# Keeping a token's row and its upsampled row side by side in DRAM, and adding them only after the gather

## The chip, the cores and the metric

The kernel runs on one core of a Trainium2 chip. The metric is the device time of one execution in microseconds (us); a single number is the median of several runs. PE is TensorE, DVE is VectorE, ACT is ScalarE, POOL is GpSimd, and SP is the engine whose queue issues most DMAs (SPq).

## The reference

Two stages, cut to what matters:

```
# q, k, v: (8 batches, 8 heads, 576 positions, 64)
q_d, k_d, v_d = means over groups of 4 positions                 # 144 positions
out_up    = repeat(softmax(q_d k_d^T / 8) v_d, 4, axis=positions)
out_local = softmax(q k^T / 8 where |i - j| < 4) v
x = (out_up + out_local) as (4608 tokens, 512)

logits = x @ w_gate                                              # 8 experts
# all (token, expert) pairs in falling order of logit; a token goes to the first
# expert that still has one of its 576 places
out[tokens of e] = relu(x[tokens of e] @ w1[e]) @ w2[e]          # 512 -> 1024 -> 512
```

`out_up` has only 144 different rows per batch: four neighbouring tokens share one. The gate is linear, so the logits of `x` are those of `out_local` plus those of `out_up`.

## The kernel before

**Attention.** The 4608 tokens are 36 tiles `u` of 128 tokens (4.5 tiles per batch). For a tile, `loc_s`, `loc_t` and `loc_v` compute the local attention with PE, and `norm` leaves it in SBUF as `x` (128 x 512). For a batch `b`, two passes `g` of four heads compute the attention of the 144 coarse positions; their `end()` writes it to a DRAM tensor `up_dram`: 128 of the 144 rows as two DMAs (L387, one per `g`), the other 16 rows as one (L394). Later `load_up` (L416) reads, for each tile, the 32 coarse rows that it needs, each four times, into an SBUF tile `up`. `log_a` (L484) adds: `x = x + up`, on DVE for the first 28 tiles and on POOL for the last 8. `store` (L487) writes the sum to `x_dram` (4608 x 512). `log_t` transposes it on PE (L494, four 128x128 blocks in fp32) and splits it into two fp16 parts (ACT L498, DVE L499); `log_m` multiplies them with the gate's weights (L509, L512) and DVE sums the result into `lg` (L514).

The order of this stage is written out by hand: every step of tile `u` has a lag in the table `LOC`, the steps are sorted by time, and each engine gets its instructions in that order. All DMAs of the stage share SP's queue: stores, loads of `up`, the q, k and v of the next batch (`nat`, `natt`, L200 and L215) and the windows of v (`vw`, L229).

**Routing.** The token-expert assignment takes a fixed number of threshold searches: DVE compares (L703), PE counts (L733). Those for the first expert stand between the stages, those for a later expert run beside the matmuls of the one before. Each ends with `idx`, 576 row numbers, as four columns of 128 and one of 64.

**Experts.** A scheduler orders this stage, with priorities. For an expert, `gather` lets POOL issue five indirect DMAs (L1068) that fetch rows of `x_dram` into `xg`. For the first two experts PE transposes `xg` (L1077, four blocks per 128 rows) and ACT and DVE split it into two fp16 parts `xt`; for the others ACT and DVE split first, into a tile `xs` (L1088 is DVE's part), and a DMA transposes it (L1090). The weights are split into fp16 parts too (L1053 is DVE's part). Then come the two layers, `pH` (L1105) and `pX` (L1134), and POOL scatters the rows of `y` to the output (L1143).

Of the kernel before, what the change touches and what calls it, by code (L numbers as in the profile page):

```python
# [49 lines left out]
LOC = {'up': 1.7, 'st': 4.6, 't': 1.3, 'lm': 8.07, 's0': 0.33, 's1': 0.331, 'lt': 5.61, 'v0': 1.83, 'v1': 1.831, 'add': 4.5}  # L50
# [39 lines left out]
class Attention:  # L90
    def __init__(self, ctx, tc, q, k, v, wg, ident, identb, maskc, x_dram, up_dram, lg, big, more=()):
        self.tc, self.nc = tc, tc.nc
        self.q, self.k, self.v = q, k, v
        self.x_dram, self.up_dram, self.lg = x_dram, up_dram, lg
# [22 lines left out]
        self.vw, self.vd, self.qz, self.qdz, self.qdt, self.sw, self.ptw = [], [], [], [], [], [], []  # L117
        self.sd = cst.tile([128, 9, G], F32, name="sd")
# [245 lines left out]
    def down_v(self, b, g):  # L364
# [10 lines left out]
        x = self.wk.tile([128, 5, D], F32, name="xu", bufs=2)  # L375
# [8 lines left out]
        def end():  # L384
            r = self.norm(o, x[:, :4], 4 + g, 4.0)
            up = self.up_dram[b * G:b * G + 128, 256 * g:256 * g + 256]
            nc.sync.dma_start(up, x[:, :4].rearrange("p h d -> p (h d)"))  # L387
            if g:
                own = self.wk.tile([128, 2], F32, name="own")
                nc.vector.tensor_tensor(own, r[:, 4:].to_broadcast([128, 2]), self.half, op=OP.mult)  # L390
                y = x[:, 4]
                nc.vector.tensor_scalar(y, o[:, 260:324], own[:, :1], None, op0=OP.mult)
                nc.vector.scalar_tensor_tensor(y, o[:, 325:389], own[:, 1:], y, op0=OP.mult, op1=OP.add)
                nc.sync.dma_start(bass.AP(tensor=up.tensor, offset=up.offset - 256 * g + 128 * HD,  # L394
                                          ap=[[D, H], [HD, 16], [1, D]]), y)
# [14 lines left out]
    def load_up(self, u):  # L410
        for b in {4 * u // NW, (4 * u + 3) // NW}:
            for g in range(2):
                self.need(("v", b, g))
        t = self.wk.tile([128, HD], F32, name="up", bufs=UB)
        src = self.up_dram[32 * u:32 * u + 32]
        getattr(self.nc, UPQ).dma_start(t, bass.AP(tensor=src.tensor, offset=src.offset, ap=[[HD, 32], [0, 4], [1, HD]]))  # L416
        self.up[u] = t

# [59 lines left out]
    def log_a(self, u):  # L481
        nc = self.nc
        x = self.x[u]
        (nc.gpsimd if u >= ADDU else nc.vector).tensor_tensor(x, x, self.up[u], op=OP.add)  # L484

    def store(self, u):
        getattr(self.nc, STQ).dma_start(self.x_dram[128 * u:128 * u + 128], self.x[u])  # L487

    def log_t(self, u):
        nc = self.nc  # L490
        x = self.x[u]
        p = self.ps.tile([128, 4, 128], F32, name="g", bufs=8)
        for c in range(4):
            nc.tensor.transpose(p[:, c], x[:, 128 * c:128 * c + 128], self.ident)  # L494
        xt = self.wk.tile([128, 2, 4, 128], F16, name="xt", bufs=TB)
        pf = p.rearrange("p c t -> p (c t)")
        hi = xt[:, 0].rearrange("p c t -> p (c t)")
        nc.scalar.activation(hi, pf, AF.Copy, scale=XS)  # L498
        self.after(FT, lambda: nc.vector.scalar_tensor_tensor(xt[:, 1].rearrange("p c t -> p (c t)"), pf, XS, hi,  # L499
                                                              op0=OP.mult, op1=OP.subtract), ("x", u))  # L500
        self.xt[u] = xt

    def log_m(self, u):
        nc = self.nc
        self.need(("x", u))
        xt = self.xt.pop(u)
        l = self.ps.tile([128, 2, E], F32, name="g", bufs=8)
# [6 lines left out]
        nc.vector.tensor_reduce(self.lg[:, u], l.rearrange("p s e -> p e s"), axis=AX.X, op=OP.add)  # L514
# [23 lines left out]
    def run(self, after, ready):  # L538
        self.so, self.x, self.up, self.xt, self.ptd = {}, {}, {}, {}, {}
# [13 lines left out]
        for b in range(B):  # L553
# [35 lines left out]
        for u in range(NT):  # L589
            if u > 1:  # L590
                work.append((u - VWT, 0, 0, lambda u=u: self.load_vw(u), False))
            for j, (name, lag) in enumerate(LOC.items()):
# [4 lines left out]
                if name == "up":  # L597
                    at = max(at, end[(4 * u + 3) // NW])
                work.append((at, 2, j, stage[name](u), name in PEL))
                if name == "lm" and u in SETUP:  # L600
                    steps = after(SETUP[u], u + 1)
                    work += [(at + SPACE * k, 3, k, lambda g=steps: next(g, None), False) for k in range(24)]
# [23 lines left out]
XSB = 4  # L626
# [381 lines left out]
class Experts:  # L1008
# [50 lines left out]
    def gather(self, idx, first):  # L1059
# [5 lines left out]
        for c, (s0, n) in enumerate(SL):  # L1065
            xg = self.wk.tile([128, HD], F32, name="xg", bufs=5)
# [4 lines left out]
            xgs.append(xg)  # L1071

        def piece(c):
            s0, n = SL[c]
            p = self.ps.tile([128, 4, 128], F32, name="pX", bufs=2)
            for d in range(4):
                self.turned = nc.tensor.transpose(p[:, d, :n], xgs[c][:n, 128 * d:128 * d + 128], self.ident[:n, :n])  # L1077
# [5 lines left out]
        def piece_dma(c):  # L1083
            s0, n = SL[c]
            xs = self.wk.tile([128, 2, HD], F16, name="xs", bufs=XSB)
            with self.tc.high_priority():
                nc.scalar.activation(xs[:n, 0], xgs[c][:n], AF.Copy, scale=XM)
            getattr(nc, LOE).scalar_tensor_tensor(xs[:n, 1], xgs[c][:n], XM, xs[:n, 0], op0=OP.mult, op1=OP.subtract)  # L1088
# [4 lines left out]
        return xt, piece if first else piece_dma  # L1093

    def mlp(self, w, xt, idx, in1, in2):
# [28 lines left out]
        for c, (s0, n) in enumerate(SL):  # L1124
# [13 lines left out]
            y = self.wk.tile([128, 512], F32, name="y", bufs=3)  # L1138
# [152 lines left out]
```

## Time and profile before

| | |
|---|---|
| median of 3 runs | 795.96 us (794.89 to 797.41) |
| the profiled execution | 787.11 us, of which 785.1 us are the span |
| attention, to the last logits | about 0 to 292 us of the span |
| routing for the first expert, up to its gather | 292 to 322 us |
| eight experts | 322 to 785 us |
| PE busy | 679.8 us, 87% of the span |
| DVE busy | 560.6 us, 71% |
| POOL busy | 244.6 us, 31% |

A row of the profile names the line of the kernel, the engine, the operation and its tiles (out<-in), then how often it ran, its busy time, the mean duration of one, and the idle time of its engine just before it. A row that starts with SPq is SP's DMA queue. All times within the run are on the scale of the span.

### The profile page before, as it was taken

The page shows a single profiled execution, that of the slowest core. Times are in us where ns is not written, and L with a number is a line of the kernel's source. Part 1 is how long each engine was busy: PE and PEld are TensorE (multiplying, and loading weights), DVE is VectorE, ACT ScalarE, POOL GpSimd, SP SyncE. Part 2 cuts the span into 40 slices and gives each one's busy share as a digit, 9 for nine tenths or more (in the row PEclk, how much of TensorE's full clock was granted, in tenths as well). Part 3 has the DMA queues.
Part 4 walks back from the last instruction along what each step waited for, and adds up shares of the span by engine and source line. Part 5 has one row for each costly group of instructions (what it writes and reads, how often), then busy time and mean ns, then how long its engine had stood idle before and what let it go on. Part 6 is the DMA issues. An engine that isn't in the chain of part 4 may idle for free.

```text
span 785.1 us, 21193 instructions
## 1 busy us (share of the span) xinstructions
PE 679.8 (87%) x8565; PEld 470.0 (60%) x8565; DVE 560.6 (71%) x1679; ACT 331.6 (42%) x631; POOL 244.6 (31%) x274
## 2 busy tenths in 40 slices
PE   7687988886898863399899999999999979999994
PEld 4576777675777752365466466366466456574752
DVE  7878879977797887887969979798889336171210
ACT  3357677663776440341624325144234134262210
POOL 9263455535346440300610502121320402201001
PEclk9699899998999995599999999999999989999998
DMA  9949979798999750621615555572835935404001
GB/s 258 220 132 242 255 193 287 194 262 209 226 238 214 190 178 10 196 80 51 252 34 196 139 168 171 101 257 67 257 114 215 222 120 128 108 2 100 22 27 34
DMA packets 148133, 125.00 MB, mean 159 GB/s; under 512 B 92228, under 2 KB 122436, under 8 KB 148036
## 3 DMA queue, kind: packets, MB, share of 16 engines
q1 hardware_dynamic: 140656, 102.12, 49.3%
q0 software_dynamic: 6432, 20.98, 8.8%
q8 instruction: 68, 1.11, 0.6%
q10 hardware_dynamic: 948, 0.55, 0.3%
q14 instruction: 29, 0.24, 0.1%
HBM read 95.30 MB, written 21.23 MB: 148 GB/s over the span
## 4 chain that ended last, share of the span: by engine, by line
PE 32%; DVE 23%; issue 21%; DMA 11%; ACT 5%; POOL 3%; SPq 3%; POOLq 0%; ACTq 0%; DVEq 0%
PE pH L1105 10%; PE pX L1134 5%; DVE cmp L703 2%; POOL out_dram L1143 2%; DVE wl L1053 2%; PE g L292 2%; DMA nat<-in_q_dram 2%; PE pR L733 2%; PE g L476 2%; DMA vw<-in_v_dram 2%; DMA up_dram<-xu 2%; DMA nat<-in_moe_w_dram 1%; DVE ht L1121 1%; PE g L373 1%; DMA xt<-xs 1%
## 5 line engine op out<-in xcount | busy, mean ns | idle before, releaser
L1105 PE MATMUL pH<-xt,wh 128*128 128x256 f16 (+1 forms) x1024 | 199.3, 289 | 5.4 <-DMA xt<-xs 4.7
L1134 PE MATMUL pX<-wh,ht 128*128 128x512 f16 (+1 forms) x640 | 182.4, 384 | 1.9 <-DVE xt L1081 1.9
L1105 PE MATMUL pH<-xt,wl 128*128 128x320 f16 (+1 forms) x512 | 147.7, 289 | 0.0
L1134 PEld LDWEIGHTS <-ht 128*128 128x128 f16 (+1 forms) x960 | 82.2, 101 | 90.2 <-issue 6.4
L1143 POOL DMA_INDIRECT out_dram<-y,idx x40 | 44.1, 1102 | 280.2 <-ACT y L1140 224.0
L1134 PE MATMUL pX<-wl,ht 128*128 128x512 f16 (+1 forms) x320 | 119.2, 384 | 0.0
L1105 PEld LDWEIGHTS <-wh 128*128 128x128 f16 x1024 | 98.5, 99 | 32.5 <-issue 8.3
L1118 ACT ACTIVATE ht<-pH 128x512 f16<-128x512 f32 (+1 forms) x128 | 45.5, 408 | 129.8 <-PE pH L1105 129.8
L1053 DVE SCALAR_TENSOR_TENSOR wl<-nat,wh 128x512 f16<-128x512 f32 x128 | 84.7, 682 | 2.8 <-ACT wh L1051 0.6
L1068 POOL DMA_INDIRECT xg<-x_dram,idx x40 | 49.4, 1234 | 112.0 <-DVE idx L1004 33.9
L1121 DVE SCALAR_TENSOR_TENSOR ht<-pH,ht 128x512 f16<-128x512 f32 (+1 forms) x128 | 52.5, 450 | 41.1 <-ACT ht L1118 40.7
L1140 ACT ACTIVATE y<-pX 128x512 f32<-128x512 f32 (+1 forms) x40 | 23.7, 594 | 127.0 <-PE pX L1134 82.2
L1051 ACT ACTIVATE wh<-nat 128x1024 f16<-128x1024 f32 x64 | 66.6, 1056 | 9.5 <-DMA nat<-in_moe_w_dram 9.5
L1105 PEld LDWEIGHTS <-wl 128*128 128x128 f16 x512 | 50.5, 99 | 12.4
L465 ACT COPY pt<-g 64x512 f32<-64x512 f32 x72 | 41.8, 580 | 35.5 <-PE g L454 34.4
L292 PE MATMUL g<-ident,nat 128*128 128x128 f32 x256 | 40.7, 287 | 14.7 <-DMA nat<-in_q_dram 12.3
L476 PE MATMUL g<-vw,pt 128*64 128x65 f32 x1152 | 45.4, 232 | 3.3 <-ACT pt L465 2.1
L1142 DVE SCALAR_TENSOR_TENSOR y<-pX,y 64x512 f32<-64x512 f32 x8 | 5.5, 693 | 59.2 <-ACT y L1140 59.0
L476 PEld LDWEIGHTS g<-vw,pt 128*64 128x64 f32 x1152 | 40.4, 145 | 9.4 <-ACT pt L465 5.7
L278 ACT COPY kt<-g 64x512 f32<-64x512 f32 (+1 forms) x56 | 35.1, 626 | 19.2 <-PE g L292 11.0
L265 POOL TENSOR_TENSOR gtmp<-qz 64x576 f32<-64x576 f32 x28 | 32.6, 1163 | 30.0 <-DVE kdt L268 24.7
L278 ACT COPY qz<-g 64x512 f32<-64x512 f32 (+1 forms) x52 | 33.0, 634 | 19.6 <-PE g L292 16.5
(219 smaller groups left out, 1190.3 us busy)
## 6 DMA issues: line engine op xcount, KB each, us to landing
nat<-in_moe_w_dram SPq DMA_DIRECT2D x28, 1024.0 KB
vw<-in_v_dram SPq DMA_DIRECT2D x136, 96.0 KB
up<-up_dram SPq DMA_DIRECT2D x36, 256.0 KB
x_dram<-x SPq DMA_DIRECT2D x36, 256.0 KB
nat<-in_q_dram SPq DMA_DIRECT2D x16, 512.0 KB
nat<-in_k_dram SPq DMA_DIRECT2D x16, 512.0 KB
nat<-in_v_dram SPq DMA_DIRECT2D x14, 512.0 KB
up_dram<-xu SPq DMA_DIRECT2D x16, 128.0 KB
```

What stands on the lines that cost most here:

```text
L278: self.nc.scalar.copy(out, in_)
L292: nc.tensor.transpose(p[:, a, :, fp], src[:, 4 * hh + 2 * a + s, 2 * fp:2 * fp + 2].rearrange("p f d -> p (f d)"), self.ident)
L465: self.nc.scalar.copy(out, in_)
L476: nc.tensor.matmul(o[64 * i:64 * i + 64, 65 * h:65 * h + 65], pt[:, 2 * g + i, h].rearrange("p b q -> p (b q)"), self.vw[u % 4][:, i, 4 * ...
L1051: nc.scalar.activation(hi, r, AF.Copy, scale=sc)
L1053: nc.vector.scalar_tensor_tensor(lo[:, a:a + LOP], r[:, a:a + LOP], sc, hi[:, a:a + LOP], op0=OP.mult, op1=OP.subtract)
L1068: self.fetched = nc.gpsimd.indirect_dma_start(out=xg[:n], out_offset=None, in_=self.x, in_offset=bass.IndirectOffsetOnAxis(ap=idx[:n, c:c ...
L1105: mm = nc.tensor.matmul(p[:, s, :s1 - s0], w[d][a][:, 128 * f:128 * f + 128], xt[:, b, d, s0:s1], start=j == 0, stop=j == len(seq) - 1)
L1118: last = nc.scalar.activation(hi, q, AF.Relu)
L1121: nc.vector.scalar_tensor_tensor(lo, q, 0.0, hi, op0=OP.max, op1=OP.subtract)
L1134: mm = nc.tensor.matmul(p[o:o + m], ht[:, f, h0:h0 + m], w[4 + f // 2][b][:, 512 * (f % 2):512 * (f % 2) + 512], start=j < parts, stop=j > ...
L1143: i = nc.gpsimd.indirect_dma_start(out=self.out, in_=y[:n], in_offset=None, out_offset=bass.IndirectOffsetOnAxis(ap=idx[:n, c:c + 1], axis=0))
```

## The change

A row of `x_dram` now has 1024 numbers: the local attention on the left, the upsampled row on the right. Nothing in the attention stage adds the two any more.

- The coarse attention of a batch is collected in `xu` (128 x 512) and `yu` (the last 16 rows). `up_put` writes `xu` with one DMA, each row to four tokens (1 MB), and `yu` with four DMAs. `up_dram`, `load_up` and `log_a` are gone.
- The gate is applied to the coarse rows once: `up_t` and `up_m` are `log_t` and `log_m` for the 128 rows of `xu`. The 16 rows per batch in `yu` are read back from `x_dram` in two groups, of five and three batches (`tail_get`), and go the same way. The logits go to a small DRAM tensor `lup_dram`, four copies each (`lup_put`: 32 bytes per token), and come back in the layout of `lg` with two DMAs (`lget`: tiles 0 to 23 and 24 to 35). `ladd` adds them to `lg`, the first on POOL, the second on DVE.
- The lags are new, `x` has 4 buffers instead of 6, and the first of two preparations of the routing starts two tiles earlier.
- The gather of an expert fetches 4 KB rows. For the first expert PE sums while it transposes: two fp32 matmuls with the identity per block, accumulated, in place of one transpose. For the others POOL adds the halves (128 x 512) behind the gathers. From the third expert on, `xs` lies in the right half of `xg`. The output tile `y` has 2 buffers instead of 3.

```diff
-        up = self.up_dram[b * G:b * G + 128, 256 * g:256 * g + 256]
-        nc.sync.dma_start(up, x[:, :4].rearrange("p h d -> p (h d)"))
...
+        at = d.offset + b * S * 2 * HD + HD
+        self.nc.sync.dma_start(bass.AP(tensor=d.tensor, offset=at, ap=[[8 * HD, 128], [2 * HD, 4], [1, HD]]),
+                               x[:, None].to_broadcast([128, 4, HD]))
+        for r in range(4):
+            self.nc.sync.dma_start(bass.AP(tensor=d.tensor, offset=at + (512 + r) * 2 * HD,
+                                           ap=[[D, H], [8 * HD, 16], [1, D]]), y)
...
+        self.logits_t(self.xu[b][0], ("up", b), "xtu", 2)
...
+        self.nc.sync.dma_start(bass.AP(tensor=d.tensor, offset=d.offset + at * E, ap=[[4 * E, n], [E, 4], [1, E]]),
+                               rows[:, None].to_broadcast([n, 4, E]))
...
+        (self.nc.vector if u1 == NT else self.nc.gpsimd).tensor_tensor(a, a, b, op=OP.add)
...
-        (nc.gpsimd if u >= ADDU else nc.vector).tensor_tensor(x, x, self.up[u], op=OP.add)
...
-LOC = {'up': 1.7, 'st': 4.6, 't': 1.3, 'lm': 8.07, 's0': 0.33, 's1': 0.331, 'lt': 5.61, 'v0': 1.83, 'v1': 1.831, 'add': 4.5}
+LOC = {'st': 3.4, 't': 1.3, 'lm': 5.46, 's0': 0.33, 's1': 0.331, 'lt': 3.0, 'v0': 1.83, 'v1': 1.831}
...
+            xg = self.wk.tile([128, 2 * HD], F32, name="xg", bufs=5)
...
+        if how:
+            for c, (s0, n) in enumerate(SL):
+                with self.tc.high_priority():
+                    nc.gpsimd.tensor_tensor(xgs[c][:n, :HD], xgs[c][:n, :HD], xgs[c][:n, HD:], op=OP.add)
...
+                if how == 0:
+                    nc.tensor.matmul(p[:, d, :n], cut, self.ident[:n, :n], start=True, stop=False)
+                    self.turned = nc.tensor.matmul(p[:, d, :n], xgs[c][:n, HD + 128 * d:HD + 128 * d + 128],
+                                                   self.ident[:n, :n], start=False, stop=True)
+                else:
+                    self.turned = nc.tensor.transpose(p[:, d, :n], cut, self.ident[:n, :n])
```

The lines of the changed kernel that the order below names: L532 store of `x`, L418 and L421 `up_put`, L436 `lup_put`, L205 and L220 loads of q, k and v, L234 windows of v, L1128 gather, L1135 POOL's add, L1143 and L1144 PE's sums, L793 the counts of the routing, L1175 first layer, L1213 scatter.

First place: SP's queue at a batch switch. Before, the q and k of the next batch (L200) stand behind the writes to `up_dram` and the first read of it:

```order
L487 DMA x_dram<-x 128x512
L387 DMA up_dram<-xu 128x256 x2
L394 DMA up_dram<-xu 8x16x64
L416 DMA up<-up_dram 128x1x512
L200 DMA natt<-in_q_dram 64x1x256 x2
L200 DMA natt<-in_k_dram 64x1x256 x2
L215 DMA nat<-in_q_dram 128x4x256
L215 DMA nat<-in_k_dram 128x4x256
```

The same place in SP's queue after the change:

```order
L205 DMA natt<-in_q_dram 64x1x256 x2
L205 DMA natt<-in_k_dram 64x1x256 x2
L220 DMA nat<-in_q_dram 128x4x256
L220 DMA nat<-in_k_dram 128x4x256
L234 DMA vw_129<-in_v_dram 48x8x64 x3
L234 DMA vw_129<-in_v_dram 32x8x64
L234 DMA vw_129<-in_v_dram 6x8x64
L532 DMA x_dram<-x 128x512
L220 DMA nat<-in_q_dram 128x4x256
L220 DMA nat<-in_k_dram 128x4x256
L220 DMA nat<-in_v_dram 128x4x256
L234 DMA vw_130<-in_v_dram 48x8x64 x4
```

The loads of the next batch now stand ahead of the put of the coarse rows, which follows a few DMAs later, and no DMA of SP's reads back what was just written until the tails.

Second place: PE where the first expert begins. Before, the transposes of `xg` (L1077) come in portions with the first layer between them:

```order
L994 MATMUL pR<-r,ohl 64x72
L1077 MATMUL pX<-ident,xg 128x128 x8
L1105 LDWEIGHTS wh_5834
L1105 MATMUL pH<-xt,wh_5834 128x256
L1105 LDWEIGHTS wh_5834
L1105 MATMUL pH<-xt,wh_5834 128x256
L1077 MATMUL pX<-ident,xg 128x128 x8
L1105 LDWEIGHTS wh_5834
L1105 MATMUL pH<-xt,wh_5834 128x256
```

After it, the last of the 40 summing matmuls and what follows them, on PE:

```order
L1144 MATMUL pX<-ident,xg 128x64
L1143 MATMUL pX<-ident,xg 128x64
L1144 MATMUL pX<-ident,xg 128x64
L793 LDWEIGHTS cmp_6064
L793 MATMUL pR<-oh,cmp_6064 128x16
```

All five tiles of rows are now summed, and the 18 counts of the next expert's routing made, before the first layer begins.

Third place: POOL from the end of the first expert to that of the second. Before, five gathers stand in a row, then the scatters of the expert that is ending:

```order
L1143 DMA out_dram<-y,idx 4608x512 x2
L1068 DMA xg<-x_dram,idx 128x512 x4
L1068 DMA xg<-x_dram,idx 64x512
L1143 DMA out_dram<-y,idx 4608x512 x4
L1068 DMA xg<-x_dram,idx 128x512 x4
L1068 DMA xg<-x_dram,idx 64x512
```

The same stretch of POOL's queue after the change:

```order
L1213 DMA out_dram<-y,idx 4608x512 x2
L1128 DMA xg<-x_dram,idx 128x1024 x4
L1135 TENSOR_TENSOR xg<-xg 128x512
L1128 DMA xg<-x_dram,idx 64x1024
L1135 TENSOR_TENSOR xg<-xg 128x512 x3
L1213 DMA out_dram<-y,idx 4608x512
L1135 TENSOR_TENSOR xg<-xg 64x512
L1213 DMA out_dram<-y,idx 4608x512 x3
```

Each add waits for its gather to land, and the next gather's issue and the scatters wait behind it.

More of the change, by code (lines that the diff above doesn't have):

```diff
@@ L90, with __init__ @@
 class Attention:
-    def __init__(self, ctx, tc, q, k, v, wg, ident, identb, maskc, x_dram, up_dram, lg, big, more=()):
+    def __init__(self, ctx, tc, q, k, v, wg, ident, identb, maskc, x_dram, lup_dram, lg, big, more=()):
         self.tc, self.nc = tc, tc.nc
         self.q, self.k, self.v = q, k, v
-        self.x_dram, self.up_dram, self.lg = x_dram, up_dram, lg
+        self.x_dram, self.lup_dram, self.lg = x_dram, lup_dram, lg
         nc = self.nc
@@ L408, in norm, with up_put @@
         return r
[L410 to L417, printed above, removed]
+    def up_put(self, b):
+        for g in range(2):
+            self.need(("v", b, g))
+        x, y = self.xu[b]
+        d = self.x_dram
+        at = d.offset + b * S * 2 * HD + HD
[4 more added lines that the diff above has]
+                                           ap=[[D, H], [8 * HD, 16], [1, D]]), y)
@@ new lines, in up_t, with up_m, lup_put @@
+    def up_t(self, b):
+        for g in range(2):
+            self.need(("v", b, g))
+        self.logits_t(self.xu[b][0], ("up", b), "xtu", 2)
+    def up_m(self, b):
+        self.lup[b] = self.wk.tile([128, E], F32, name="lup")
+        self.logits_m(self.lup[b], ("up", b))
+    def lup_put(self, rows, at):
+        d = self.lup_dram
+        n = rows.shape[0]
+        self.nc.sync.dma_start(bass.AP(tensor=d.tensor, offset=d.offset + at * E, ap=[[4 * E, n], [E, 4], [1, E]]),
+                               rows[:, None].to_broadcast([n, 4, E]))
@@ new lines, in up_lput, with tail_get, tail_t @@
+    def up_lput(self, b):
+        self.lup_put(self.lup[b], b * S)
+    def tail_get(self, i):
+        a, b = TAILS[i]
+        d = self.x_dram
+        t = self.wk.tile([128, HD], F32, name="tail", bufs=1)[:16 * (b - a)]
+        self.nc.sync.dma_start(t, bass.AP(tensor=d.tensor, offset=d.offset + (a * S + 512) * 2 * HD + HD,
+                                          ap=[[S * 2 * HD, b - a], [8 * HD, 16], [1, HD]]))
+        self.tail = t
+    def tail_t(self, i):
+        self.logits_t(self.tail, ("tail", i), "xtu", 2)
@@ new lines, in tail_m, with tail_lput, lget @@
+    def tail_m(self, i):
+        a, b = TAILS[i]
+        self.tail = self.wk.tile([128, E], F32, name="lup")[:16 * (b - a)]
+        self.logits_m(self.tail, ("tail", i))
+    def tail_lput(self, i):
+        a, b = TAILS[i]
+        for c in range(a, b):
+            self.lup_put(self.tail[16 * (c - a):16 * (c - a) + 16], c * S + 512)
+    def lget(self, u0, u1):
+        d = self.lup_dram
+        self.nc.sync.dma_start(self.lgu[:, u0:u1], bass.AP(tensor=d.tensor, offset=d.offset + 128 * u0 * E,
+                                                           ap=[[E, 128], [128 * E, u1 - u0], [1, E]]))
@@ L596, in run, with more @@
                     at += max(E0 - u * E1, 0.0) - max(u - UE, 0) * CE * int(lag - 1)
-                if name == "up":
-                    at = max(at, end[(4 * u + 3) // NW])
                 work.append((at, 2, j, stage[name](u), name in PEL))
+                if name == "lm":
+                    lmt = at
                 if name == "lm" and u in SETUP:
                     steps = after(SETUP[u], u + 1)
-                    work += [(at + SPACE * k, 3, k, lambda g=steps: next(g, None), False) for k in range(24)]
+                    work += [(at + SETLAG[u] + SPACE * k, 3, k, lambda g=steps: next(g, None), False) for k in range(24)]
+        def more(at, n, f, pe):
+            work.append((at, 2, n, f, pe))
+        for b in range(B):
+            for k, lag in UP[b].items():
+                more(end[b] + lag, 100, lambda f=getattr(self, "up_" + k), b=b: f(b), k in "tm")
+        for i, lags in enumerate(TAIL):
+            for k, lag in lags.items():
+                more(end[TAILS[i][1] - 1] + lag, 101, lambda f=getattr(self, "tail_" + k), i=i: f(i), k in "tm")
+        for b, u0, u1, l0, l1 in LGET:
+            more(end[b] + l0, 102, lambda a=(u0, u1): self.lget(*a), False)
+            more(max(end[b] + l1, u1 == NT and lmt + 0.1), 103, lambda a=(u0, u1): self.ladd(*a), False)
         work.sort(key=lambda z: z[:3])
@@ L1057, in split, with gather @@
         return w, piece
-    def gather(self, idx, first):
+    def gather(self, idx, how):
         nc = self.nc
```

93 lines of the change are left out of this document (48 added, 45 removed).

## The prediction

> **What bounds the kernel now.** I read the busy times first, then the stages in windows, then the waits and the chain at the places where the change lies. The columns of a window are its length, the busy time of PE, weight loads, DVE, ACT and POOL (with counts), then PE's granted clock, the DMA engines' share and GB/s.
>
> ```profile
> PE 679.8 (87%) x8565; PEld 470.0 (60%) x8565; DVE 560.6 (71%) x1679; ACT 331.6 (42%) x631; POOL 244.6 (31%) x274
> ```
>
> ```profile
> 60.00:100.00 40.00, 34.32 (x736) 29.62 (x734) 33.06 (x86) 27.00 (x55) 17.00 (x21) 0.91 0.99 252
> 100.00:140.00 40.00, 35.99 (x842) 31.51 (x840) 33.70 (x90) 28.76 (x55) 22.37 (x29) 1.00 0.94 239
> 140.00:180.00 40.00, 33.21 (x763) 28.30 (x765) 33.53 (x86) 24.92 (x50) 19.12 (x24) 0.96 0.94 230
> 180.00:220.00 40.00, 30.56 (x698) 26.57 (x691) 30.51 (x77) 21.30 (x43) 19.51 (x26) 0.91 0.85 207
> 220.00:260.00 40.00, 35.30 (x826) 30.33 (x824) 33.28 (x90) 26.59 (x51) 21.69 (x28) 0.96 1.01 234
> ...
> 292.00:330.00 38.00, 10.99 (x133) 8.48 (x134) 29.23 (x117) 7.18 (x10) 6.25 (x6) 0.51 0.27 85
> ```
>
> From 60 to 260 us, the body of the attention stage, no engine is full: PE is busy 169.4 of 200 us, DVE 164.1, and the DMA engines' share is 0.946 on average. Three resources within 15% of each other means that taking work from one gives back only part of it. Between 292 and 330 us PE's clock is granted at half.
>
> ```profile
> 371.00:430.60 59.60, 56.44 (x450) 34.21 (x449) 50.37 (x168) 24.64 (x45) 15.97 (x9) 0.97 0.45 164
> 430.60:489.90 59.30, 57.03 (x485) 33.74 (x485) 53.30 (x179) 25.44 (x45) 17.66 (x15) 1.00 0.57 166
> 489.90:549.20 59.30, 56.75 (x493) 33.66 (x492) 51.02 (x176) 20.23 (x38) 11.51 (x10) 1.00 0.51 140
> 549.20:606.60 57.40, 56.56 (x466) 33.23 (x464) 50.92 (x201) 20.23 (x38) 11.37 (x10) 1.00 0.58 198
> 606.60:662.70 56.10, 50.87 (x332) 31.15 (x331) 26.21 (x55) 18.85 (x35) 12.70 (x12) 0.94 0.59 147
> ```
>
> A window here is about one expert's period. PE sets the pace (57.03 of 59.30 us), and until 606 us DVE is only 6 to 9 us behind it. POOL is nearly empty. A gather that comes later is free only while PE still has work in its queue.
>
> **The change, body of the attention (60 to 272 us).** Removed and added work is priced by these rows; the last row is a real fp32 product on PE, the L494 row fp32 transposes.
>
> ```profile
> L484 DVE TENSOR_TENSOR x<-x,up 128x512 f32<-128x512 f32 x28 | 28.8, 1029 | 7.9 <-DMA up<-up_dram 7.9
> L499 DVE SCALAR_TENSOR_TENSOR xt<-g,xt 128x512 f16<-128x512 f32 x36 | 24.5, 682 | 3.2 <-ACT xt L498 3.1
> L494 PE MATMUL g<-ident,x 128*128 128x128 f32 x144 | 24.0, 291 | 1.3 <-POOL x L484 1.3
> L498 ACT ACTIVATE xt<-g 128x512 f16<-128x512 f32 x36 | 21.5, 597 | 8.8 <-PE g L494 8.3
> L484 POOL TENSOR_TENSOR x<-x,up 128x512 f32<-128x512 f32 x8 | 10.1, 1271 | 3.3 <-DMA up<-up_dram 2.1 <-DMA x_dram<-x 1.1
> L509 PE MATMUL g<-wg,xt 128*128 128x16 f16 x144 | 9.1, 172 | 0.9 <-ACT qz L278 0.6 <-ACT xt L498 0.3
> ...
> L476 PE MATMUL g<-vw,pt 128*64 128x65 f32 x1152 | 45.4, 232 | 3.3 <-ACT pt L465 2.1 <-DMA x_dram<-x 0.9 <-issue 0.3
> ```
>
> Removed: 28 adds on DVE, 28.8 us, and 8 on POOL, 10.1 us. Added: ten more sets of logits (eight batches, two tails). A set costs PE four transposes, 24.0/36 = 0.67 us, and eight products, of which four are 9.1/36 = 0.25 us, so 0.5 us; ACT 0.6 us; DVE 0.68 us and a small sum. In all PE +11.7, ACT +6, DVE +8.5 us. DVE thus loses a net 20 us of 164, PE gains 12 on 169. PE would have to fill 94% of a body that is 8 us shorter, against 85% now; I don't expect that much.
>
> The wait that goes away is SP's:
>
> ```profile
> SPq L416 <- DMA up_dram<-xu: 13.5, 10, 2.9
> ...
> PE g L292 <- DMA nat<-in_q_dram: 10.0, 3, 6.3
> ```
>
> ```profile
> 109.53 2.64 DMA up_dram<-xu
> 112.22 0.53 SPq L416
> 112.80 0.59 SPq L200
> ...
> 115.35 4.88 DMA nat<-in_q_dram
> 120.36 0.63 PE g L292 x4
> ```
>
> The columns of the first are total, count and longest. SP's queue stands behind the landing of the coarse rows before it may read them, and the next batch's q comes after that: in the chain 2.64 us of landing, then issues, then 4.88 us of transfer, then PE. In the new order q and k stand ahead of the put, and nothing is read back. So most of PE's 10.0 us for q should go; each of the three waits becomes a wait for something else soon (DVE, ACT's exponentials), as the balanced busy times say.
>
> Bytes hardly change:
>
> ```profile
> up<-up_dram SPq DMA_DIRECT2D x36, 256.0 KB
> ```
>
> These 36 reads and 2.3 MB of puts go; eight puts of 1 MB and four of 32 KB per batch come. New are 9216 packets of 32 bytes for the logits; I cost them at 0 to 6 us, the upper end by the packet records of the gate weights' load (9.6 ns each, shared by 16 engines). With the share at 0.946 the body cannot shrink by more than 11 us of its 200. The upper end is PE's 12 us with a third of them uncovered, +4. I take **-5 us** (-12 to +4), below the middle of the ends because PE's added work sits on the busiest engine.
>
> **End of the attention.**
>
> ```profile
> 274.61 1.72 DMA up_dram<-xu
> 276.72 2.63 DMA up<-up_dram
> ...
> 280.99 4.08 DMA up<-up_dram
> ...
> 286.52 2.38 DMA x_dram<-x
> 288.98 1.27 POOL x L484
> 290.30 0.67 PE g L494 x4
> ...
> 292.72 1.83 DVE cmp L703 x3
> ```
>
> Before, from the last coarse rows to the last logits is 274.61 to about 292.3 us, 17.7 us: put, two reads, an add that waits for a buffer, one set of logits. Now the links are: five puts (about 3 us of issue), 2 to 4 us landing, `tail_get` 2.6 to 4.1 us, a set of logits 0.67 + 0.61 + 0.70 + 0.6 = 2.6 us, three `lup_put`s (1.6 us of issue and 2 to 2.5 landing), `lget` 3 to 4 us, `ladd` 0.5 us: 17.3 to 22 us, middle 19.7. The tail is read back in a chain where it was a chain before; only the links differ. I take **+2 us** (-3 to +6: the cases are that the local tiles end later anyway, or that each landing takes the 4.08 us of the slow one).
>
> **First expert.** All its rows are behind the path: PE waits for the gather.
>
> ```profile
> 328.28 1.13 PE pX L1077 x4
> ...
> 330.66 1.81 PE pX L1077 x8
> ```
>
> Four transposes at the half clock take 0.9 us (1.81/2). A fp32 product of 64 outputs and 65 columns takes 45.4/1152 = 0.039 us in the L476 row; four of these make a 128x128 block, 0.158 us, or 0.32 at the half clock. A tile of 128 rows, eight products, then takes 2.5 us instead of 0.9 at the half clock, and 1.3 us at the full one. For four and a half tiles that is +7.2 us cold and, against 0.45 us, +3.7 us warm; some of it lies in the wait for the later gathers. Besides, the first layer starts only when all five are done, while today 12 of its matmuls run in between, and the 18 counts go ahead; they are work that would come anyway. Rows of twice the size land later by up to 1 us. I take **+4 us** (+1 to +7).
>
> [...]
>
> **Second expert.** POOL's adds stand between gathers and PE's transposes.
>
> ```profile
> L1068 POOL DMA_INDIRECT xg<-x_dram,idx x5: 947/1469/4152, 379.4 to 389.3; - x5
> ...
> 388.85 4.29 PE pX L1134 x24
> ```
>
> The last of five gathers starts at 389.3. The first add, at 1.27 us from the POOL row above, ends at 390.3, then the last gather issues (1.5 us), and the second add ends at 393.1. PE needs the first two tiles before L1134 goes on; that was 388.85 and would be 393.6, +4.7 us. PE however comes 4 us later already, so the two are one delay in part. I take **+2 us** more (0, all covered, to +5, routing late too).
>
> **Third expert and later.** The adds are 4 x 1.27 + 1.27 = 6.4 us of POOL per expert, on an engine that is busy 18 of 59 us. They lie ahead of ACT's and DVE's split, which today waits for DVE anyway. What they may cost is DVE's speed:
>
> ```profile
> L484 DVE TENSOR_TENSOR x<-x,up x28: 679/918/1707, 62.9 to 258.4; 128x512 f32<-128x512 f32 x28
> ...
> L1053 DVE SCALAR_TENSOR_TENSOR wl<-nat,wh 128x512 f16<-128x512 f32 x80 | 53.7, 679 | 0.7 <-ACT wh L1051 0.3
> ```
>
> The add that reads two SBUF tensors lasts 679 ns at best and 1707 at worst in the attention stage, where POOL computes beside it; the L499 row, one input of which is in PSUM, has 682 on average. L1053 is like the add, at its floor of 679 because POOL computes nothing beside it today. With 6.4 us of POOL at 1 - 679/1707 = 60% lost, DVE loses up to 3.8 us per expert, less than the 6 us by which it trails in the 430.60 row; where its result is due in that moment it shows. I take **+1 us** over all (0 to +6).
>
> [...]
>
> **The sum.** -5 + 2 + 4 + 2 + 1 = +4 us, on the profiled 787.11 us that is 791.1; on the median of 795.96, which is 8.9 us above the profiled execution, 800 us. The attention's part is what I trust least.
>
> **Rivals.**
> 1. *Faster*: the body was held by SP's queue alone. For it: SP's 13.5 us of waits, PE's 10.0 us for q, and the DMA share that falls to 0.85 in the 180 row. Against: PE's added 12 us. Body -12, end 0, first expert +2, the rest 0 to +1: -9.5, 786.5 us. It decides when PE's waits for q vanish without others.
> 2. *Even*: the body gains 8 us, and the experts give them back, within 0.3% (793.6 to 798.3 us), which is about what a measurement of this kernel can tell from no change: 796 us.
> 3. *Clearly slower by contention*: DVE becomes the bound in experts 2 to 5. It trails by 6.0 us in the 430.60 row; with 3.8 us of lost speed and the compares and splits waiting in line, half of the 6.4 us of each of four experts shows: +13 in place of +1, 812 us. It decides from 6 us of loss per expert.
> 4. *The fp32 sums cost more*: if the L476 products run in pairs, one per half of the outputs, a block costs twice 0.158 us; 18 blocks of two such products against one transpose are 18 x (0.63 - 0.11) = 9.4 us warm and 18.8 cold: +12 in place of +4, 808 us. The counterweight is that part of PE's time there is waiting for gathers.
>
> **How the numbers follow.** The forecast's case, slower by 3 to 9 us, has 0.30; rival 1 has 0.34; rival 2 has 0.20; rival 3 has 0.10; rival 4 has 0.06. Slower by over 0.3% is 0.30 + 0.10 + 0.06 = 0.46. Faster and slower are near each other, so the range holds both: it starts below rival 1's 786.5, at 784, since the body's -12 may come with nothing lost, and ends at rival 3's 812. The likeliest case by itself reaches from 798.3 to 805.
>
> **What would show it.** Right: in the attention no wait of SP's for coarse rows, q's waits of PE under 3 us, DVE some 20 us less busy to 292 us with PE some 12 us more; PE's L1143 and L1144 together near 6 to 10 us; the first pX of the second expert about 5 us later against its idx; L1053 over 700 ns on average. Wrong: an attention stage shorter by more than 12 us, DMA packets of 32 bytes with a landing over 4 us in the chain, or DVE's L1053 above 900 ns.

## The result, and the profile after

The changed kernel takes 829.69 us (median of 4 runs, 819.44 to 832.36) against 795.42 us: a ratio of 1.0383, with a 95% interval of 1.0288 to 1.0479. It is slower by some 34 us, where 4 were forecast. The profiled execution took 829.55 us with a span of 827.9 us, 42.8 us longer than the span of before. The ratio leaves out the changed kernel's run of 832.36 us, a slow one that lies over 1.5% above its fastest, and it is not the quotient of the two medians. The 42.8 us are more than the 34 because the profiled execution of the kernel before (787.11 us) was 8.3 us quicker than the median of its runs; a difference of two traces below is one of two executions.

Where this lies is read from three moments in the two traces: the row numbers `idx` of the first expert, the last `pX` matmul of the first expert, and that of the eighth.

| | before | changed | difference |
|---|---|---|---|
| start to the first expert's row numbers | 321.5 us | 327.3 us | +5.8 |
| from there to the end of the first expert's `pX` | 71.6 us | 85.5 us | +13.9 |
| from there to the end of the eighth's | 381.8 us | 404.9 us | +23.1 |

The busy times of the page of the changed kernel, in the same form as before:

```profile
PE 702.5 (85%) x8745; PEld 489.5 (59%) x8745; DVE 569.8 (69%) x1672; ACT 335.4 (41%) x641; POOL 274.3 (33%) x302
```

DVE lost 28 adds and yet is busy 9 us more: time in which an instruction waits in the engine counts as busy here, as the 5.26 us of a threshold below show, which took 0.19 us at the median. The windows of the changed kernel, the first five in the attention stage, the last three from the end of one expert's `pX` to that of the next (experts 2 to 4), and the last three of the kernel before for comparison below them:

```profile
60.00:100.00 40.00, 35.15 (x790) 30.80 (x791) 32.13 (x88) 27.88 (x57) 15.43 (x21) 0.96 0.95 248
100.00:140.00 40.00, 35.69 (x790) 31.72 (x789) 28.78 (x82) 28.23 (x55) 20.83 (x28) 1.00 0.78 209
140.00:180.00 40.00, 34.03 (x812) 29.89 (x811) 31.19 (x88) 26.73 (x53) 16.57 (x24) 0.94 0.96 242
180.00:220.00 40.00, 36.40 (x844) 31.95 (x842) 31.48 (x90) 25.22 (x50) 22.51 (x31) 0.93 0.91 240
220.00:260.00 40.00, 32.38 (x717) 28.01 (x713) 24.31 (x70) 24.49 (x47) 18.70 (x27) 0.96 0.77 189
412.80:483.30 70.50, 62.93 (x530) 35.62 (x531) 60.04 (x184) 22.32 (x41) 19.79 (x17) 0.95 0.41 127
483.30:548.40 65.10, 58.82 (x453) 33.06 (x453) 56.60 (x193) 20.59 (x40) 17.28 (x15) 0.95 0.50 148
548.40:614.20 65.80, 58.87 (x488) 34.40 (x488) 57.11 (x179) 21.20 (x42) 21.12 (x18) 0.97 0.61 203
```

```profile
393.10:455.30 62.20, 59.96 (x528) 35.29 (x526) 50.13 (x178) 22.13 (x41) 13.52 (x12) 1.00 0.44 132
455.30:514.00 58.70, 56.26 (x457) 32.74 (x457) 50.62 (x194) 20.52 (x40) 11.18 (x10) 1.00 0.51 141
514.00:572.50 58.50, 57.14 (x487) 33.81 (x488) 51.88 (x180) 21.16 (x42) 15.69 (x13) 1.00 0.63 206
```

In the attention stage DVE is busy 147.9 us of 200 instead of 164.1 and the DMA engines' share fell from 0.946 to 0.874, but the last product of PE for the tiles' own logits ends at 293.84 us, against 292.62 before: the stage did not end earlier. In the experts DVE is busy 5 to 10 us more per period, and a period is 6 to 8 us longer. PE's own busy time grew too, from 173.4 to 180.6 us over the three periods with about the same number of products; its granted clock, the column after POOL's, is 0.95 to 0.97 there instead of 1.00. The longer busy time is a third of the 22 us by which the three periods grew. Which DVE instructions grew is seen in the groups of DVE from expert 2 on, first of the changed kernel (390 to 660 us), then the same of the kernel before (371 to 627 us):

```profile
L1113 DVE SCALAR_TENSOR_TENSOR wl<-nat,wh 128x512 f16<-128x512 f32 x77 | 59.8, 781 | 0.3
L763 DVE TENSOR_TENSOR cmp<-xh,thr 128x512 bf16<-128x512 int16 x10 | 12.4, 1236 | 0.0
L815 DVE SCALAR_TENSOR_TENSOR thr<-nj,rest 128x32 int16<-128x32 f32 x10 | 9.2, 921 | 0.2
```

```profile
L1053 DVE SCALAR_TENSOR_TENSOR wl<-nat,wh 128x512 f16<-128x512 f32 x80 | 53.7, 679 | 0.7 <-ACT wh L1051 0.3
L703 DVE TENSOR_TENSOR cmp<-xh,thr 128x512 bf16<-128x512 int16 x10 | 4.2, 420 | 0.0
L755 DVE SCALAR_TENSOR_TENSOR thr<-nj,rest 128x32 int16<-128x32 f32 x10 | 1.9, 188 | 0.2
```

A mean of 921 ns for an instruction that took 188 in the kernel before hides a few very long ones. The longest of them in order of time (start, duration), DVE first, then POOL at the same moment:

```profile
567.83 0.17 DVE L811 TENSOR_REDUCE nj<-pR 128x1 f32<-128x8 f32 x1 [0.25 <-PE pR L809]
568.03 5.26 DVE L815 SCALAR_TENSOR_TENSOR thr<-nj,rest 128x32 int16<-128x32 f32 x1
573.21 0.68 DVE L1191 SCALAR_TENSOR_TENSOR ht<-pH,ht 128x512 f16<-128x512 f32 x1
```

```profile
567.12 1.19 POOL L1128 DMA_INDIRECT xg<-x_dram,idx  x1 [0.15 <-POOL xg L1135]
568.32 4.91 POOL L1135 TENSOR_TENSOR xg<-xg 128x512 f32<-128x512 f32 x4
```

DVE's threshold over 128x32 numbers stands for 5.26 us, until POOL's fourth add in a row ends at 573.2 us. It is not slowed by a share: it waits for all four. Among the DVE instructions that overlap with POOL's adds in experts 2 to 8, all that stood have both inputs in SBUF: ten of L1113 took 0.9 us longer on average than their shortest, five of L763 1.7 us, four of L815 2.1 us, one of L958 0.9 us. Fourteen that read PSUM (L801, L807, L811, L969, L1151, L1191, L1212) lost 0.02 us at most. Not every one with both inputs in SBUF stood: L822, 128x1, took 0.16 us at 618.32 us, while two adds ran (616.95 to 619.61 us). The threshold is a link in the routing chain (DVE threshold, DVE compare, PE count), so PE waits too. The waits of PE while the experts run, of the changed kernel (349 to 671 us) and of before (330 to 627 us):

```profile
PE pR L793 <- DVE cmp L763: 14.7, 7, 4.9
```

```profile
PE pR L733 <- DVE cmp L703: 3.6, 4, 1.7
```

### The profile page after: what moved, and what is told of

Same layout as the page of the kernel before. It is cut to its first block, busy times and chain, and to the rows that moved or that the text cites. A ratio compares the mean times of both kernels' runs of the same rounds, so it can differ in the third digit from the quotient of the medians.

```text
span 827.9 us, 21558 instructions
## 1 busy us (share of the span) xinstructions
PE 702.5 (85%) x8745; PEld 489.5 (59%) x8745; DVE 569.8 (69%) x1672; ACT 335.4 (41%) x641; POOL 274.3 (33%) x302
## 4 chain that ended last, share of the span: by engine, by line
PE 43%; DVE 23%; issue 14%; DMA 7%; POOL 6%; ACT 5%; SPq 1%; POOLq 0%; ACTq 0%; DVEq 0%
PE pH L1175 14%; PE pX L1204 11%; DVE cmp L763 3%; PE g L526 3%; DVE wl L1113 2%; PE g L378 2%; PE pR L793 2%; DMA xt<-xg 2%; DVE ht L1191 2%; PE g L297 1%; PE g L545 1%; POOL xg L1128 1%; DVE thr L815 1%; DMA xg<-x_dram,idx 1%; ACT pt L515 1%
## 5 line engine op out<-in xcount | busy, mean ns | idle before, releaser
L1175 PE MATMUL pH<-xt,wh 128*128 128x256 f16 (+1 forms) x1024 | 198.3, 289 | 3.8 <-DVE ht L1191 3.2
L1204 PE MATMUL pX<-wh,ht 128*128 128x512 f16 (+1 forms) x640 | 185.1, 388 | 0.0
L1175 PE MATMUL pH<-xt,wl 128*128 128x320 f16 (+1 forms) x512 | 147.6, 289 | 0.0
L1213 POOL DMA_INDIRECT out_dram<-y,idx x40 | 44.9, 1122 | 258.7 <-ACT y L1210 240.7
L1175 PEld LDWEIGHTS <-wh 128*128 128x128 f16 x1024 | 97.8, 98 | 30.3 <-DVE ht L1191 3.9
L1113 DVE SCALAR_TENSOR_TENSOR wl<-nat,wh 128x512 f16<-128x512 f32 x128 | 93.8, 752 | 6.9 <-ACT wh L1111 5.2
L1128 POOL DMA_INDIRECT xg<-x_dram,idx x40 | 51.0, 1276 | 142.1 <-DMA nat<-in_moe_w_dram 65.2
L1210 ACT ACTIVATE y<-pX 128x512 f32<-128x512 f32 (+1 forms) x40 | 23.8, 594 | 151.9 <-PE pX L1204 85.5
L1191 DVE SCALAR_TENSOR_TENSOR ht<-pH,ht 128x512 f16<-128x512 f32 (+1 forms) x128 | 52.5, 451 | 28.4 <-ACT ht L1188 27.9
L1175 PEld LDWEIGHTS <-wl 128*128 128x128 f16 x512 | 50.3, 98 | 12.5 <-issue 0.2
L1212 DVE SCALAR_TENSOR_TENSOR y<-pX,y 64x512 f32<-64x512 f32 x8 | 5.5, 694 | 69.0 <-ACT y L1210 68.9
L1135 POOL TENSOR_TENSOR xg<-xg 128x512 f32<-128x512 f32 (+1 forms) x35 | 45.0, 1294 | 13.9 <-DMA xg<-x_dram,idx 13.3
L793 PEld LDWEIGHTS <-cmp 128*128 128x128 bf16 x504 | 19.3, 98 | 44.3 <-DVE cmp L763 29.0
```

The costliest lines, as they stand in the source:

```text
L1113: nc.vector.scalar_tensor_tensor(lo[:, a:a + LOP], r[:, a:a + LOP], sc, hi[:, a:a + LOP], op0=OP.mult, op1=OP.subtract)
L1128: self.fetched = nc.gpsimd.indirect_dma_start(out=xg[:n], out_offset=None, in_=self.x, in_offset=bass.IndirectOffsetOnAxis(ap=idx[:n, c:c ...
L1135: nc.gpsimd.tensor_tensor(xgs[c][:n, :HD], xgs[c][:n, :HD], xgs[c][:n, HD:], op=OP.add)
L1175: mm = nc.tensor.matmul(p[:, s, :s1 - s0], w[d][a][:, 128 * f:128 * f + 128], xt[:, b, d, s0:s1], start=j == 0, stop=j == len(seq) - 1)
L1191: nc.vector.scalar_tensor_tensor(lo, q, 0.0, hi, op0=OP.max, op1=OP.subtract)
L1204: mm = nc.tensor.matmul(p[o:o + m], ht[:, f, h0:h0 + m], w[4 + f // 2][b][:, 512 * (f % 2):512 * (f % 2) + 512], start=j < parts, stop=j > ...
```

## The experiments

Names that begin with b are the kernel before with something added, those with a the changed kernel with something taken away. Each ratio is to the kernel before on the same chip. Theory A is what the trace above suggests: DVE's instructions with both inputs in SBUF wait until POOL's adds end, for all of several in a row (5.26 us for four).

**POOL's adds put into the kernel before.** Behind the gathers of experts 2 to 8:

```diff
+            for c, (s0, n) in enumerate(SL):
+                with self.tc.high_priority():
+                    v = xgs[c][:n].rearrange("p (a d) -> p a d", a=4)
+                    nc.gpsimd.tensor_tensor(v, v, self.zero[:n, None].to_broadcast([n, 4, 128]), op=OP.add)
```

By theory A some +15 us (+10 to +22) were expected, with thresholds of 1 to 5 us and over 10 us of waits of PE for the compares.

> The kernel before with one thing added: behind the five gathers of experts 2 to 8, POOL adds a tile of zeros to each gathered tile (35 adds of about 1.27 us), and everything else as it was. [...] Theory B (the adds are innocent, the larger rows and the new order of instructions cost the time): within 4 us of the kernel before.

Measured: 825.52 us against 792.32, ratio 1.0446 (1.0375 to 1.0516). With nothing else of the change, the adds cost as much as the whole change does, and more than theory A's +10 to +22 us. Theory B falls.

**The adds without anyone who waits for them.** In the kernel before, behind the gathers of experts 2 to 8 again: POOL adds each gathered tile to itself, into a tile that nobody reads, and `y` has two buffers:

```diff
+                    nc.gpsimd.tensor_tensor(self.zero[:n], xgs[c][:n], xgs[c][:n], op=OP.add)
```

The other reading of `b_pool` is that the splits and transposes wait for the adds' results and that nothing else costs: then this run loses little, and the next most of what `b_pool` lost.

> [...] Theory A, POOL's add holds back DVE: most of what b_pool lost (35 us over 792) is lost here too, +15 to +35 us, with DVE instructions of 2 to 7 us. [...]

Measured: 810.62 us against 792.25, ratio 1.0249 (1.0179 to 1.0318), some 20 us. Its groups of DVE from expert 2 on (371 to 660 us) show the same three instructions stretched:

```profile
L1054 DVE SCALAR_TENSOR_TENSOR wl<-nat,wh 128x512 f16<-128x512 f32 x81 | 65.9, 821 | 0.5 <-ACT wh L1052 0.3
L703 DVE TENSOR_TENSOR cmp<-xh,thr 128x512 bf16<-128x512 int16 x10 | 6.4, 643 | 0.0
L755 DVE SCALAR_TENSOR_TENSOR thr<-nj,rest 128x32 int16<-128x32 f32 x10 | 3.5, 354 | 0.2
```

So, by the middle of the two ratios, somewhat more than half of what `b_pool` lost is lost with work whose result nobody uses. The adds' place in POOL's queue is part of that; the next run prices it.

**The waits without the adds.** The same place in POOL's queue as in `b_pool`, 16 of 512 columns:

```diff
+                    v = xgs[c][:n].rearrange("p (a d) -> p a d", a=4)[:, :, :4]
+                    nc.gpsimd.tensor_tensor(v, v, self.zero[:n, None, :4].to_broadcast([n, 4, 4]), op=OP.add)
```

> The kernel before; behind the gathers of experts 2 to 8 POOL adds zeros to only 16 of the 512 columns of each gathered tile, in place: the same place in POOL's queue, the same waits for the gather and for POOL's result, but an add of about 0.1 us. Theory A: 0 to +6 us. [...]

Measured: 795.59 us against 792.25, ratio 1.0053 (1.0019 to 1.0088), some 4 us. The waits for the gathers' landing and for POOL's result, and the scatters behind, are cheap; what is dear is the time for which an add runs. Theory A stands, and the other reading, by which this run would have lost most of what `b_pool` did, falls. That `b_pool` lost some 15 us more than `b_off` is most simply read as the price of waiting for a full add's result, which theory A had not named; the two kernels also differ in the form of the add and in the buffers of `y`, so this is not shown.

**The adds on DVE.** In the changed kernel:

```diff
-                    nc.gpsimd.tensor_tensor(xgs[c][:n, :HD], xgs[c][:n, :HD], xgs[c][:n, HD:], op=OP.add)
+                    nc.vector.tensor_tensor(xgs[c][:n, :HD], xgs[c][:n, :HD], xgs[c][:n, HD:], op=OP.add)
```

> The changed kernel with the 35 adds of experts 2 to 8 on DVE instead of POOL. Theory A: the waits of DVE go, and its own 35 x 0.68 = 24 us of adds come in their place, part of it in gaps: 813 to 822 us instead of 830, no DVE instruction stretched, L1113 back at 0.68 us. Theory B: DVE has more to do and nothing is won, 830 to 840 us.

Measured: 821.39 us against 792.32, ratio 1.0401 (1.0325 to 1.0476), no better than the changed kernel's 1.0383. One half of theory A came: no threshold takes over 0.2 us any more, and the splits are back at 678 ns (390 to 660 us):

```profile
L1113 DVE SCALAR_TENSOR_TENSOR wl<-nat,wh 128x512 f16<-128x512 f32 x77 | 52.0, 678 | 0.1
```

The gain that it forecast was a miss: it had counted DVE's own adds but not that DVE now stands before gathers that have not landed, for 17.4 us in all. DVE's waits in the same stretch (total, count, longest):

```profile
DVE xg L1135 <- DMA xg<-x_dram,idx: 17.4, 14, 3.7
```

**No adds at all.** The loop with the adds is left out:

```diff
-        if how:
-            for c, (s0, n) in enumerate(SL):
-                with self.tc.high_priority():
-                    nc.gpsimd.tensor_tensor(xgs[c][:n, :HD], xgs[c][:n, :HD], xgs[c][:n, HD:], op=OP.add)
```

> The changed kernel without the adds of experts 2 to 8 (these experts see only the left halves of the rows; gathers of 4 KB rows, PE's sums for the first expert and the whole attention stay). Theory A: 808 to 815 us, periods of experts 2 to 4 as in the kernel before (58 to 62 us). Theory B: 824 us or more.

Measured: 800.37 us against 792.32, ratio 1.0091 (1.0054 to 1.0128), better than theory A's 808 to 815 us. The experts from the second on see only the left halves of the rows. From the first expert's end to the eighth's it needs 379.5 us, less than the 381.8 of before. Its periods of experts 2 to 4 are 58.5 to 60.9 us, as before, with a granted clock of 0.97 to 1.00. Of the change's 3.8%, 2.9 points are the adds.

**The attention stage alone.** The upsampled rows go to a tensor of their own, the expert stage is that of before:

```diff
+        xu_dram = dr.tile([NTOK, HD], F32, name="xu_dram")
...
-        at = d.offset + b * S * 2 * HD + HD
+        at = d.offset + b * S * HD
...
-                xt, piece = ex.gather(idx, 0)
+                xt, piece = ex.gather(idx, True)
```

> The changed kernel's attention stage and gate, with the upsampled rows in a DRAM tensor of their own, and the expert stage of the kernel before (2 KB rows of the local attention alone; the experts do not see the upsampled rows). It shows what the attention stage by itself costs or brings. From the two traces (the first expert's row numbers come 5.8 us later, 321.5 to 327.3): 800 to 803 us. If the attention stage is no worse and that lateness is chance of one execution: 793 to 797 us.

Measured: 794.83 us against 792.32, ratio 1.0009 (0.9967 to 1.0051): the attention stage brings nothing and costs nothing that can be measured.

**No sums on PE in the first expert**, on top of the kernel without adds:

```diff
-                xt, piece = ex.gather(idx, 0)
+                xt, piece = ex.gather(idx, 1)
```

> The changed kernel without POOL's adds, and with the first expert's 40 fp32 products replaced by 20 transposes of the left halves (4 KB gathers stay; the experts do not see the upsampled rows). Against a_noadd (800.4 us, 1.009 of before) it shows what PE's sums cost. From the trace of the changed kernel, where PE's 40 products last from 337.9 to 349.4 us: 5 to 7 us less, 794 to 796 us. If the PE time hides behind the later gathers: within 2 us of a_noadd.

Measured: ratio 1.0072 (1.0041 to 1.0104), within 2 us of 1.0091, as the second reading said. The traces show a difference (76.1 instead of 81.6 us from the row numbers to the end of the first expert), but the runs do not resolve it. Beside `a_sep`'s 1.0009 some 5 us are left, with the 4 KB gathers and the two buffers of `y` still in; no run separates these.

**Work for POOL before the first gather**, on top of the kernel without adds. The first gather's issue is long in every kernel with the new attention stage (POOL's timeline of the changed kernel and of before):

```profile
328.25 6.38 POOL L1128 DMA_INDIRECT xg<-x_dram,idx  x1 [65.16 <-DMA nat<-in_moe_w_dram]
```

```profile
322.53 1.52 POOL L1068 DMA_INDIRECT xg<-x_dram,idx  x1 [32.29 <-DMA nat<-in_moe_w_dram]
```

```diff
-        (self.nc.vector if u1 == NT else self.nc.gpsimd).tensor_tensor(a, a, b, op=OP.add)
+        self.nc.gpsimd.tensor_tensor(a, a, b, op=OP.add)
```

> The changed kernel without the adds of experts 2 to 8, and with the second addition of logits (128 x 96) on POOL instead of DVE. In the four kernels with the new attention stage the first gather's issue lasts 6.4 us, in those with the old one 1.5 us; in the old ones POOL has worked 32 us before, in the new ones 65 us before. Theory D, POOL has to start up again after a long rest: with work 30 us before the gather, its issue is back at 1.5 us and the kernel 3 to 5 us faster than a_noadd, 796 to 798 us. Theory E, DVE's work at that moment (the splits of the weights) holds POOL's gather back: the issue still lasts 6 us.

Measured: the issue lasts 6.3 us although POOL worked 30 us before it, so theory D falls. The ratio is 1.0162 (1.0102 to 1.0222), above the 1.0091 without the edit, though the intervals overlap; I have no reason for it.

**The changed kernel once more.**

> The changed kernel once more, beside the same runs of the kernel before as the kernel without the tail. The first gather's issue lasts 6.4 us again and ends 1.0 us behind DVE's last two-input instruction (L870), as in the other five kernels with the new attention stage; the ratio to the kernel before is 1.035 to 1.045. If the long first gather was chance: 1.5 us in this execution.

Measured: 829.20 us against 796.77, ratio 1.0433 (1.0388 to 1.0478); the issue lasts 6.38 us again. In the seven traced kernels with this stage so far, and in the one without the tail below, it starts 0.32 to 0.41 us into the first of eight splits of the weights (L1113, two inputs in SBUF) and ends 1.01 to 1.02 us behind the last two-input instruction of that run (L870). In the four with the old stage it starts 0.25 us into the first split and lasts 1.5 us.

**One-input instructions in between.** Eight of them among the splits, in `a_sep` and in the changed kernel. If the splits hold the first gather back, which is theory E, it should get in between them:

```diff
+                if first and k < 4:
+                    nc.vector.tensor_reduce(self.wk.tile([128, 1], F32, name="gap"), lo[:, a:a + 64], axis=AX.X, op=OP.max)
```

> a_sep with eight small one-input DVE instructions (a maximum over 64 numbers that nobody reads) between the first expert's splits of the weights, which are two-input instructions and follow one another without a break while the first gather issues. [...] If the long issue has another cause: 6.4 us again, or 1.0 us behind L870 wherever that ends.

> The same eight small one-input DVE instructions in the changed kernel. Theory E: first gather's issue 1.5 to 3 us, first expert 4 to 5 us earlier against its row numbers, 1.033 to 1.039 of before instead of 1.038 to 1.043. Otherwise no change.

Measured: the issue lasts 2.25 us in `a_gap` and 2.24 us in the changed kernel, so theory E stands. The timeline of `a_gap`, POOL and DVE:

```profile
329.90 2.25 POOL L1131 DMA_INDIRECT xg<-x_dram,idx  x1 [64.97 <-DMA nat<-in_moe_w_dram]
```

```profile
330.89 0.19 DVE L1015 TENSOR_TENSOR asg<-asg,n 128x36 f32<-128x36 f32 x1
331.00 0.34 DVE L1117 TENSOR_REDUCE gap<-wl 128x1 f32<-128x64 f16 x2
331.25 1.28 DVE L1114 SCALAR_TENSOR_TENSOR wl<-nat,wh 128x512 f16<-128x512 f32 x2
```

The issue ends at 332.15 us, 1.15 us behind the start of the first pair of one-input instructions (331.00 us), while DVE is still splitting. In time, `a_gap` is at 1.0003 (0.9976 to 1.0031) beside `a_sep`'s 1.0009, no difference, and the changed kernel with it at 1.0345 (1.0291 to 1.0399), on the fast side of the 1.0383 and 1.0433 without, but the intervals overlap. Between their row numbers and the first expert's end the traces show 73.5 us in `a_gap` beside 74.2 in `a_sep`, and 82.2 in the changed kernel beside 85.5 and 86.0 without: less than the 4 to 5 us that were expected.

**No tail**, on top of `a_sep`: the 16 last coarse rows of each batch are not read back, and their logits are taken from other rows:

```diff
-TAIL = ({"get": 2.4, "t": 3.6, "m": 4.4, "lput": 5.3}, {"get": 0.9, "t": 2.75, "m": 3.65, "lput": 4.0})
+TAIL = ({"lput": 5.3}, {"lput": 2.2})
```

> a_sep (new attention stage, upsampled rows in their own tensor, expert stage of the kernel before) without the read-back of the 16 last coarse rows per batch: their logits are taken from other rows, so the routing differs a little. No tail_get, no logits for the tails; the copies to lup_dram and lget follow the last batch's coarse logits at once. In six executions each, the row numbers of the first expert came 6 us later with the new attention stage than with the old one while the last logits of local tiles came at the same time. If the tail's chain is that lateness: row numbers at 321 to 324 us and 4 to 7 us less than a_sep, 0.992 to 0.997 of the kernel before. If the body sets the end anyway: no change, 1.00.

Measured: the first row numbers come at 318.4 us in the profiled execution (330.6 in that of `a_sep`), but the ratio is 0.9993 (0.9959 to 1.0026), not different from `a_sep`. With other logits the experts' routing is another one, and its expert stage was 10 us longer, so this run does not settle what the tail costs.

## Why the prediction was wrong

**The step that failed is "third expert and later", +1 us.** The row 679/918/1707 was read as a loss of speed, 60% while POOL runs, at most 3.8 us per expert and hidden in the 6 us by which DVE's busy time stays under a period. The runs showed a wait: DVE instructions with two inputs in SBUF stood until POOL's add ended, or four of them in a row, 5.26 us for one that takes 0.19. The trace of before had this already, at one of the longest adds of that row (DVE, then POOL):

```profile
117.40 1.70 DVE L484 TENSOR_TENSOR x<-x,up 128x512 f32<-128x512 f32 x1
```

```profile
117.28 1.27 POOL L241 TENSOR_TENSOR gtv<-nat 128x512 f32<-128x512 f32 x1
```

DVE's add ends 0.55 us behind POOL's: hardly any of its 679 ns was done while POOL's ran. The slack did not hide it, since the waits fell on the chain of thresholds, compares and counts on which PE depends: the adds cost 2.9 points, about 23 us (1.0383 against 1.0091; 404.9 against 379.5 us in the traces). PE's waits for compares grew by 11 us; its busy time at the lower granted clock grew by some 7 us in three periods. The traces with full adds on POOL (changed kernel, `b_pool`, `b_off`) have a clock of 0.95 to 0.97 in all of these periods; those without (before, `a_noadd`, `b_tiny`) have 1.00 in seven of nine and 0.97 in two. So the clock goes with the waits, but no run separates the two. Of the rivals, 3 is the nearest, the same contention in the same place, at 23 us instead of its 13; its way, DVE as the bound, did not come (60.04 of 70.50 us busy). The prediction's sign of being wrong here, L1053 above 900 ns on average, did not come either: its mean from expert 2 on (L1113 now) is 781 ns.

By their recorded starts DVE's instruction, at 568.03 us, was ahead of POOL's first add, at 568.32, and yet it waited for four adds; but POOL was busy with a gather's issue from 567.12 to 568.31 us, so this does not tell which of the two came first. What the two have to share is not shown by any run either; the runs show the wait alone.

**Second expert, +2 us.** Its place was right: in the changed kernel's trace PE waits 4.8 and 1.3 us for adds before the transposes. From the row numbers to the first expert's end, the changed kernel's 85.5 us stand against 81.6 without adds: 3.9 us, within the bounds of 0 to 5. (In its working, 389.3 + 1.27 is 390.6 and not 390.3, a slip of 0.3 us.)

**First expert, +4 us (+1 to +7).** Without POOL's adds the interval grew from 71.6 to 81.6 us, 10 us. `a_gap` and `a_sep`, whose first expert is that of before, need 73.5 and 74.2 us for it, so some of the 10 may lie between executions. By the ratios, `a_noadd` (1.0091) stands 6.5 us above `a_sep` (1.0009). Two parts were sized wrongly. The products: each is recorded as two pieces, and the rows of PE from 326 to 352 us have

```profile
L1143 PE MATMUL pX<-ident,xg 128*128 128x128 f32 (+1 forms) x40 | 9.4, 323 | 11.7 <-DMA xg<-x_dram,idx 11.7
L1144 PE MATMUL pX<-ident,xg 128*128 128x128 f32 (+1 forms) x40 | 9.0, 312 | 0.0
```

In the chain one product takes 0.43 us at the half clock (0.50 granted from 337 to 340 us) and 0.22 at the full one (1.00 from 344 to 350), 11.7 us for all 40; I had 0.32 and 0.16. The price came from a miscount: the L476 row has 1152 records, but the kernel issues 16 of these products per tile, 576 in all, so each of them too is recorded twice and takes 0.079 us, not 0.039. Read rightly, four of them would have made 0.32 us of a block at the full clock, above the 0.22 that were measured; this is the price of rival 4. Between the traces of `a_noadd` and `a_noadd_tr` the products are 5.5 us at the end of the expert. The first of them starts 3.24 us behind the end of the first gather's issue, and the first transpose of before 2.42 us behind it: 0.8 us more with the larger rows, within the up to 1 us that was allowed for their landing. The other part, 4.9 us by which the first gather's issue is longer (6.38 instead of 1.52), was in no step; `a_gap`, where 4.1 us of it are gone, ends its first expert only 0.7 us earlier, counted from the row numbers, than `a_sep`. In the time of all runs neither is resolved by itself.

**Body, -5 us, and end, +2 us.** The mechanism was right and the gain was not: SP's waits for coarse rows went, PE's waits for q fell from 10.0 us to under 0.7, DVE lost 16 us of 164 there, and still PE's last product for the tiles' logits came 1.2 us later. SP now waits for PE instead, for buffers of `vw` (40 to 300 us):

```profile
SPq L234 <- PE g L526: 30.1, 12, 7.2
```

So neither DVE's work nor the queue's wait for coarse rows was what held the stage. Its chain through PE and ACT is what is left, PE having 4.3 us more work in these 200; that it is this chain is read from the waits, and no run tested it. The end had the right links, in the chain of the changed kernel:

```profile
277.70 3.61 DMA x_dram<-yu
...
293.05 1.75 DMA lup_dram<-lup
294.82 3.28 DMA lgu<-lup_dram
298.54 1.76 DVE cmp L763 x3
```

The compares start 5.8 us later than before (292.72), at the upper bound of +6. Over the profiled executions the row numbers came at 318.5 to 325.6 us in four with the old stage and at 321.6 to 334.3 in nine with the new one and its tail; in the runs of `a_sep` nothing is left of that. The lower bound of the body, -12 us, lay beyond the 11 us that the prediction's own sum of the DMA share allows.

**The range.** It ended at rival 3's 812 us, with rivals 3 and 4 priced each by itself. Both came, in larger or smaller part, and the gather's wait with them. The chances leaned the other way: rival 1, faster, had 0.34, more than the forecast's own case, and rival 3 had 0.10.

## What to carry to other kernels

POOL's elementwise work was not free beside DVE here, though POOL was idle 69% of the time before: 35 adds of 1.29 us on average cost 2.9 points. Count for each add its full duration as a possible stop of a DVE instruction that reads two tensors in SBUF, as the 5.26 us for four adds in a row show, and look at which DVE instruction will stand in it; if that is a link of a chain on which PE waits, slack on average did not hide it here. In a profile, look at the maximum of a DVE group beside its minimum: 679 to 1707 ns with POOL next to it was the sign, and it meant waiting, not slowness. In a row of PE, compare the number of records with the number of products that the kernel issues before dividing. A wait the other way fits what was seen of the first gather, which POOL issues while DVE runs two-input instructions: 6.38 us without a break among these, 2.24 with one-input instructions in between.

## What the runs showed of the hardware

The first gather's issue took 1.5 us in the four traces where it started 0.25 us into DVE's first split, and 6.3 to 6.4 us in the eight where it started 0.32 to 0.41 us into it: there it ended 1.01 to 1.02 us after the whole run of two-input instructions was over. Whether that tenth of a microsecond decides it is not shown, since no run moved the start alone. With one-input DVE instructions among the splits it took 2.25 us (`a_gap`) and 2.24 us (`after_gap`). Why the later gather of the kernel before, which issued among the same splits, took only 1.48 us stays open.
